# Transposing q and k of seven late units by the DMA instead of on TensorE

## The chip, the cores and the metric

One core of one Trainium2 chip. The metric is the device time of one execution in microseconds (us), lower is better. All times below are from runs of the fast state; where a kernel's time is given it is the median of its runs, and ratios to the kernel before come from runs of the same rounds on the same chip.

## The reference

Two blocks in series. A retention layer gives x, and a SiLU layer with two weight matrices takes it to the output. Everything is float32.

```
q, k, v: (batch 4, heads 8, seq 768, head_dim 64)
for t in range(S):
    state = gamma * state + outer(k[:, :, t], v[:, :, t])
    y[:, :, t] = scale * q[:, :, t] @ state
x = y as (3072 tokens, 512)
h = x @ w_in                 # (512, 2048)
out = (h * sigmoid(h)) @ w_out   # (2048, 512)
```

## The kernel before

The sequence is cut in 6 chunks of 128 tokens. A chunk of one batch is a *unit*: 24 units, numbered 0 to 23. For each unit a *visit* does the retention part in chunk form, with small matmuls that need q and k with head_dim on the partitions. So each visit begins by transposing q and k on TensorE, four 128x128 blocks each, and ScalarE copies them from PSUM:

```
def stage_t(n):                    # TensorE transposes k and q of unit n
    for name, to, bufs, src, tp in (("kt", kt, 2, kqv["k"][n], turn(...)),
                                    ("qt", qt, 3, kqv["q"].pop(n), banks("q", ...))):
        for a in range(HP):        # HP = 4 pairs of heads
            nc.tensor.transpose(tp[:, a, :], src[:, 2 * a : 2 * a + 2, :], ident)
        to[n] = one.tile([128, HP, C], FP32, ...)
        evac[:] = [nc.scalar.copy(out=to[n], in_=tp).ins]
```

Between the visits stand the *products*, h = x @ w_in for one chunk and one block of 128 columns of w_in: 96 in all, each 12 matmuls of 512 columns. ScalarE evacuates the first PSUM bank of a product (`ha`) into `hs`, VectorE subtracts the second (`hb`), ScalarE applies Silu, and SyncE sends `hs` to DRAM. There are three `hs` buffers:

```
hpool = pool("hpool", 3)
...
def product_in(c, f):
    ha, hb = turn(f"ha_{c}_{f}"), turn(f"hb_{c}_{f}")      # three banks in turn
    ... 12 matmuls ...
    hs = hpool.tile([128, NT], FP32, tag="hs", name=f"g_{c}_{f}")
    copied[:] = [nc.scalar.activation(out=hs, in_=ha, func=AF.Copy, scale=ONE_E).ins]
    ... what stands in behind_copy is placed here, on ScalarE's queue ...
    taken_out[:] = [nc.vector.tensor_tensor(out=hs, in0=hs, in1=hb, op=ALU.subtract).ins]
    ...
    nc.scalar.activation(out=hs, in_=hs, func=AF.Silu)
    pending.append((c, f, hs))

def put_g(keep):                    # the store of a product
    while len(pending) > keep:
        c, f, g = pending.pop(0)
        nc.sync.dma_start(out=g_dram[c, f], in_=g)

for n, (c, f) in enumerate(steps):
    product_in(c, f)
    if (c, f) in takes:
        take_w(...)                 # rounds a piece of w_out and stores it: load wf, store wod
    put_g(1)
    behind.get((c, f), lambda: None)()     # here the visits, one every four products later on
```

All loads and stores of this part are issued by SyncE, which takes them in one order. It is not always that of the text: a transfer that waits for nothing can stand far ahead of its place.

## Time and profile before

| | before |
|---|---|
| time, median of 4 runs | 634.22 us (632.36 to 634.83) |
| span of the profiled run | 633.9 us |
| TensorE busy, idle | 610.8, 23.1 us |
| DMA issues on SyncE, 209 to 321 us | 76, together 39.3 us of 112 (35%) |
| DMA packets of the run, those under 512 bytes | 123,215; 80,016 |

The lines behind these are in the prediction below.

### The profile page before, as it was taken

How to read it: one execution, taken by the hardware profiler on the slowest of the kernel's cores; microseconds unless marked ns; L12 is line 12 of the kernel's file. 1: busy time of each engine (PE TensorE's matmuls, PEld its weight loads, DVE VectorE, ACT ScalarE, POOL GpSimd, SP SyncE). 2: the span in 40 equal slices, each digit the busy share in tenths (PEclk: the TensorE clock that was granted, in tenths of full speed). 3: DMA queues.
4: the chain of work that ended last, by engine and by line, in shares of the span. 5: the costliest groups of instructions: out<-in, count | busy, mean ns of one | idle time of the engine just before them, and what ended most of it. 6: DMA issues, size and time to landing. Idle time of an engine off the chain costs nothing.

```text
span 633.9 us, 13555 instructions
## 1 busy us (share of the span) xinstructions
PE 610.8 (96%) x5440; PEld 506.1 (80%) x5440; DVE 420.9 (66%) x732; ACT 303.8 (48%) x583; POOL 7.1 (1%) x65
## 2 busy tenths in 40 slices
PE   5798999999999999999999999999999999999997
PEld 3686788887888888888888888888888888888785
DVE  2798897798968778687777675463645544554631
ACT  5568796676655546555467761221312221412311
POOL 3000000000000000000000000000000000000000
PEclk9989999999999999999999999999999999999999
DMA  9996886446667687775657644242433423342301
GB/s 197 213 203 174 214 228 228 166 149 200 201 196 205 177 239 224 210 218 189 231 188 216 207 139 132 100 159 73 157 109 98 170 75 124 133 131 90 112 0 67
DMA packets 123215, 103.65 MB, mean 164 GB/s; under 512 B 80016, under 2 KB 88464, under 8 KB 123152
## 3 DMA queue, kind: packets, MB, share of 16 engines
q1 hardware_dynamic: 120272, 97.54, 53.0%
q10 hardware_dynamic: 2880, 5.24, 2.2%
q8 instruction: 43, 0.70, 0.5%
q14 instruction: 20, 0.16, 0.1%
HBM read 66.06 MB, written 36.70 MB: 162 GB/s over the span
## 4 chain that ended last, share of the span: by engine, by line
PE 87%; DVE 4%; SPq 4%; DMA 2%; issue 1%; ACT 1%; DVEq 0%; ACTq 0%; POOLq 0%
PE ha L551 25%; PE o L696 20%; PE oa L696 14%; PE hb L551 13%; PE ob L696 7%; PE y L428 3%; SPq L145 3%; PE sc L395 1%; PE sc L385 1%; PE qp L369 1%; PE kp L369 1%; DMA gd<-g 1%; DMA kqv<-in_q_dram 1%; DMA wod<-cw 1%; SPq L167 0%
## 5 line engine op out<-in xcount | busy, mean ns | idle before, releaser
L551 PE MATMUL ha<-xt,wi 128*128 128x512 f32 x768 | 192.3, 392 | 0.4 <-ACT xt L475 0.4
L551 PEld LDWEIGHTS ha<-xt,wi 128*128 128x128 f32 x768 | 142.7, 188 | 31.0 <-ACT xt L475 0.5
L696 PE MATMUL o<-wo,gs 128*128 128x512 f32 x576 | 146.2, 389 | 0.0
L696 PEld LDWEIGHTS o<-wo,gs 128*128 128x128 f32 x576 | 108.1, 188 | 22.4
L608 DVE TENSOR_TENSOR gs<-gr,gs 128x512 fp32r<-128x512 f32 x96 | 62.1, 686 | 91.0 <-ACT gs L606 91.0
L696 PE MATMUL oa<-wo,gs 128*128 128x512 f32 x384 | 118.3, 389 | 0.0
L606 ACT ACTIVATE gs<-gr 128x512 fp32r<-128x512 f32 x96 | 53.4, 621 | 134.9 <-issue 132.5
L551 PE MATMUL hb<-xt,wi 128*128 128x512 f32 x384 | 103.2, 390 | 0.3 <-ACT g L555 0.2
L559 DVE TENSOR_TENSOR g<-g,hb 128x512 f32<-128x512 f32 x96 | 65.7, 684 | 42.0 <-ACT g L555 28.8
L551 PEld LDWEIGHTS hb<-xt,wi 128*128 128x128 f32 x384 | 71.7, 188 | 16.5 <-ACT g L555 1.0
L696 PEld LDWEIGHTS oa<-wo,gs 128*128 128x128 f32 x384 | 72.1, 188 | 14.9
L563 ACT ACTIVATE g<-g 128x512 f32<-128x512 f32 x96 | 60.6, 631 | 48.5 <-DVE g L559 48.2
L696 PE MATMUL ob<-wo,gs 128*128 128x512 f32 x192 | 75.3, 392 | 0.3 <-DVE o L705 0.3
L555 ACT ACTIVATE g<-ha 128x512 f32<-128x512 f32 x96 | 56.9, 593 | 32.5 <-PE ha L551 21.7
L609 DVE SCALAR_TENSOR_TENSOR gs<-gs 128x512 fp32r<-128x512 f32 x96 | 62.0, 684 | 0.0
L696 PEld LDWEIGHTS ob<-wo,gs 128*128 128x128 f32 x192 | 36.0, 188 | 9.3 <-DVE o L705 2.0
L193 ACT ACTIVATE ca<-wf 128x512 f32<-128x512 f32 x32 | 21.6, 676 | 9.5 <-DVE cs L200 4.6
L403 DVE TENSOR_TENSOR am<-sc,decay 128x512 f32<-128x512 f32 x24 | 16.5, 687 | 13.9 <-PE sc L395 13.7
L428 PE MATMUL y<-qt,mid 64*64 64x64 f32 x384 | 22.6, 231 | 1.9 <-issue 1.9
L200 DVE SCALAR_TENSOR_TENSOR cs<-ca,cs 128x512 uint32<-128x512 uint32 x32 | 22.1, 691 | 0.9
L204 DVE SCALAR_TENSOR_TENSOR cp<-wf,cp 128x512 f32<-128x512 uint32 x32 | 22.1, 689 | 0.6
L704 ACT ACTIVATE o<-o 128x512 f32<-128x512 f32 x10 | 6.0, 600 | 33.1 <-PE o L696 32.7
(80 smaller groups left out, 542.2 us busy)
## 6 DMA issues: line engine op xcount, KB each, us to landing
gd<-g SPq DMA_DIRECT2D x96, 256.0 KB, 3.1
gr<-gd SPq DMA_DIRECT2D x96, 256.0 KB, 2.8
wf<-in_moe_w_out_dram SPq DMA_DIRECT2D x16, 512.0 KB, 4.3
out_dram<-o ACTq DMA_DIRECT2D x20, 256.0 KB, 2.1
wf<-in_moe_w_in_dram SPq DMA_DIRECT2D x16, 256.0 KB, 3.6
wf<-in_moe_w_in_dram SPq DMA_DIRECT2D x32, 128.0 KB, 4.1
kf<-in_k_dram SPq DMA_DIRECT2D x16, 256.0 KB, 5.0
qf<-in_q_dram SPq DMA_DIRECT2D x16, 256.0 KB, 4.5
```

What stands on the lines that cost most here:

```text
L193: nc.scalar.activation(out=a.bitcast(FP32), in_=hi.bitcast(FP32), func=AF.Abs, scale=65536.0)
L200: nc.vector.scalar_tensor_tensor(out=s, in0=a, scalar=3, in1=s, op0=ALU.logical_shift_left, op1=ALU.bitwise_or)
L204: nc.vector.scalar_tensor_tensor(out=p.bitcast(FP32), in0=lo, scalar=2.0 ** -52, in1=p.bitcast(FP32), op0=ALU.mult, op1=ALU.mult)
L428: i = nc.tensor.matmul(yp[ts(e, D), o, a, :], lhsT=lhsT, rhs=rhs, start=(e, o) not in started, stop=True, skip_group_check=True).ins
L551: nc.tensor.matmul(hb if i == 2 else ha, lhsT=w_sb[f][:, i, ts(kk, 128)], rhs=xt[c][:, i, kk, :], start=kk == 0 and i != 1, stop=kk == KIN ...
L555: copied[:] = [nc.scalar.activation(out=hs, in_=ha, func=AF.Copy, scale=ONE_E).ins]
L559: taken_out[:] = [nc.vector.tensor_tensor(out=hs, in0=hs, in1=hb, op=ALU.subtract).ins]
L563: nc.scalar.activation(out=hs, in_=hs, func=AF.Silu)
L606: nc.scalar.activation(out=t[:, 0, :], in_=g, func=AF.Copy, scale=HALF)
L608: nc.vector.tensor_tensor(out=t[:, 1, :], in0=g, in1=high, op=ALU.subtract)
L609: nc.vector.scalar_tensor_tensor(out=t[:, 2, :], in0=t[:, 1, :].bitcast(FP32), scalar=-1.0 / EPS, in1=high, op0=ALU.mult, op1=ALU.add)
L696: nc.tensor.matmul(o, lhsT=g, rhs=wo[f][:, i, :], start=first_ and i != 1, stop=last and i != 0)
```

## The change

The intent is to take 56 transposes from the engine that bounds the kernel. For units 17 to 23, q and k go another way: gathered in DRAM (eight products ahead in the text; in the trace SyncE issues the gathers between 57.9 and 138.4 us), transposed by the DMA as 16-bit words two products ahead (a float32 has two of them, so each word plane ends in its own partitions), put in order by eight small SBUF-to-SBUF copies ("reorders"), and joined by a strided copy of 16-bit words on ScalarE, q's two products later and k's three. The load of q goes; k is still loaded as well, since other matmuls take it untransposed. Two tiles hold the transposed words (the tag `qf`), one for q and one for k.

```
+    def gather_t(n):
+        for name, src in (("q", q), ("k", k)):
+            t = dram.tile([128, H, D], FP32, ...)
+            nc.sync.dma_start(out=t, in_=src[b, :, ds(c * C, C)].rearrange("h t d -> t h d"))
+    def fetch_t(n):
+        for name in "qk":
+            t = ld.tile([128, H, C], U16, tag="qf", name=f"{name}w_{n}", bufs=2)
+            nc.sync.dma_start_transpose(
+                out=t, in_=rows.pop((name, n)).bitcast(U16).rearrange("t h w -> t (h w)"))
+    def order_t(n):
+        for name in "qk":
+            src = words.pop((name, n)).rearrange("p (a j) t -> p j a t", j=2)
+            t = ld.tile([128, 2, HP, C], U16, tag="kf", name=f"{name}p_{n}", bufs=3)
+            for w in range(2):
+                for j in range(2):
+                    nc.sync.dma_start(out=t[ts(j, D), w], in_=src[w::2, j])
+    def join_t(name, n):
+        nc.scalar.copy(out=to[n].bitcast(U16).rearrange("p a (t w) -> p w a t", w=2),
+                       in_=planes.pop((name, n)))
...
-        if first:
+        if first and m < FAR:                  # FAR = 17
             stage_t(m)
...
+        if n - 2 in far:                       # far: the products with the visits of 17 to 23
+            behind_copy.append(lambda m=far[n - 2]: join_t("q", m))
+        if n - 3 in far:
+            behind_copy.append(lambda m=far[n - 3]: join_t("k", m))
+            behind_next.append(lambda m=far[n - 3]: scale_k(m))
         product_in(c, f)
         ...
         put_g(1)
         behind.get((c, f), lambda: None)()
+        if n in far:
+            order_t(far[n])
+        if n + 2 in far:
+            fetch_t(far[n + 2])
+        if n + 8 in far:
+            gather_t(far[n + 8])
```

More of the change, by code (lines that the diff above doesn't have):

```diff
@@ L15 @@
 U32 = mybir.dt.uint32
+U16 = mybir.dt.uint16
 AF = mybir.ActivationFunctionType
@@ L129 @@
     EARLY = 2 * B
+    FAR = 4 * B + 1
     early = {}
@@ L360, in scale_q @@
         nc.vector.tensor_tensor(out=t, in0=t, in1=g, op=ALU.mult)
+    rows, words, planes = {}, {}, {}
+    def gather_t(n):
+        c, b = units[n]
+        for name, src in (("q", q), ("k", k)):
+            t = dram.tile([128, H, D], FP32, tag=f"{name}{n}", name=f"{name}d_{n}")
+            nc.sync.dma_start(out=t, in_=src[b, :, ds(c * C, C)].rearrange("h t d -> t h d"))
+            rows[name, n] = t
+    def fetch_t(n):
[3 more added lines that the diff above has]
+                out=t, in_=rows.pop((name, n)).bitcast(U16).rearrange("t h w -> t (h w)"))
+            words[name, n] = t
+    def order_t(n):
[5 more added lines that the diff above has]
+                    nc.sync.dma_start(out=t[ts(j, D), w], in_=src[w::2, j])
+            planes[name, n] = t
+    def join_t(name, n):
+        to, bufs = (qt, 3) if name == "q" else (kt, 2)
+        to[n] = one.tile([128, HP, C], FP32, tag=f"{name}t", name=f"{name}t_{n}", bufs=bufs)
+        nc.scalar.copy(out=to[n].bitcast(U16).rearrange("p a (t w) -> p w a t", w=2),
+                       in_=planes.pop((name, n)))
     def stage_t(n):
@@ L529, in visit @@
             first_chunk()
-        if first:
+        if first and m < FAR:
             scale_k(m)
@@ L535, in visit @@
         for name, n in (("k", m + 2), ("q", m + 2), ("v", m + 1)):
-            if n >= EARLY:
+            if n >= EARLY and (n < FAR or name == "v"):
                 load(name, n)
+        if m >= FAR:
+            load("k", m)
         if EARLY - 2 <= m < 3 * B + 2:
@@ L653 @@
     behind[1, NF - 1] = lambda: [late_x(3), visit(EARLY + 6)]
+    far = {steps.index(x): EARLY + 6 + i for i, x in enumerate(at)
+           if FAR <= EARLY + 6 + i < len(units)}
     for n, (c, f) in enumerate(steps):
+        if n - 2 in far:
[3 more added lines that the diff above has]
+            behind_next.append(lambda m=far[n - 3]: scale_k(m))
         product_in(c, f)
```

## The prediction

> **What bounds the kernel now.** I read the page's busy shares first, then a table of windows over the region that the change touches, then the chain of waits through one period, then the groups of the operations that go, and last the DMA and the waits. The page:
>
> ```profile
> PE 610.8 (96%) x5440; PEld 506.1 (80%) x5440; DVE 420.9 (66%) x732; ACT 303.8 (48%) x583; POOL 7.1 (1%) x65
> ...
> DMA  9996886446667687775657644242433423342301
> ```
>
> TensorE is busy 96% of the span; every other engine has room on average. An average hides stages, so the windows (us, then PE, PEld, DVE, ACT, POOL busy, clock, DMA share, GB/s):
>
> ```profile
> 0.00:30.00 30.00, 19.39 (x448) 15.68 (x448) 14.67 (x27) 17.01 (x44) 5.18 (x44) 0.94 1.05 203
> ...
> 209.00:223.00 14.00, 14.00 (x185) 11.86 (x184) 10.09 (x20) 6.94 (x12) 0.09 (x1) 1.00 0.62 190
> 223.00:237.00 14.00, 14.00 (x185) 11.82 (x184) 10.17 (x19) 7.06 (x12) 0.09 (x1) 1.00 0.84 241
> ...
> 251.00:265.00 14.00, 14.00 (x170) 11.82 (x168) 9.50 (x17) 8.15 (x16) 0.09 (x1) 1.00 0.80 233
> ...
> 365.00:400.00 35.00, 35.00 (x156) 29.00 (x155) 20.14 (x33) 13.09 (x24) 0.00 (x0) 1.00 0.39 121
> ```
>
> Units 14 to 23 are staged between about 179 and 291 us (the last transpose of k starts at 288.9). There PE never idles, DVE is at 70 to 85%, ACT at 50 to 60%. The DMA engines are the second resource: 62 to 84%, mean of the six 14-us windows from 209 to 293 0.72. One period of the chain of waits (start, length, what) reads:
>
> ```profile
> 257.90 1.81 PE ha L551 x8
> 259.71 0.91 PE hb L551 x4
> 260.62 0.44 PE kp L369 x4
> 261.06 0.44 PE qp L369 x4
> 261.50 0.63 PE y L428 x32
> ```
>
> Each product is 1.81 + 0.91 = 2.72 us of matmuls, back to back; every fourth is followed by a visit of 2.96 us (260.62 to 263.58), in which the eight transposes hold 0.44 + 0.44 = 0.88 us. All is on the chain, so whatever leaves PE here leaves the span, unless a new wait comes. The groups of what goes:
>
> ```profile
> L369 PE MATMUL kp<-ident,kf 128*128 128x128 f32 x64 | 9.7, 274 | 0.0
> L369 PE MATMUL qp<-ident,qf 128*128 128x128 f32 x64 | 9.6, 273 | 0.0
> L371 ACT COPY qt<-qp 128x512 f32<-128x512 f32 x24 | 14.0, 583 | 1.4 <-PE qp L369 1.4
> L371 ACT COPY kt<-kp 128x512 f32<-128x512 f32 x24 | 14.0, 582 | 6.8 <-PE kp L369 6.7
> ```
>
> A mean of 274 ns is a latency: four cost 0.44 us on the chain, 109 ns each, since they overlap. The 0.109, not the 0.274, is what can be won. Last, what is short of slack on the DMA side:
>
> ```profile
> ACT g L555 <- DMA gd<-g: 5.7, 4, 2.2
> ...
> gd<-g SPq DMA_DIRECT2D x96, 256.0 KB, 3.1
> ...
> qf<-in_q_dram SPq DMA_DIRECT2D x16, 256.0 KB, 4.5
> ```
>
> The first line says that ScalarE, evacuating a product, already waited four times (up to 2.2 us) for the store of an older product to free one of three buffers; PE did not notice, but the margin is small.
>
> **What the Trainium skill says.** (1) "DMA: Bandwidth & Descriptors", section "Latency and other measured facts", gives a DMA transpose 261 GB/s with a non-contiguous middle dimension and about 350 to 400 when contiguous. (2) "VectorE: DVE Perf Modes", section "The three transpose paths", gives 1309 ns for one 128x128 transpose of 2-byte elements by DMA. The kernel before has no DMA transpose, so no row supports either; they disagree for a large transfer (below). (3) The first page, section "Why small descriptors are slow (HBM only)", says that 256-byte descriptors lose time to HBM but not between SBUF and SBUF. The trace agrees on HBM: the loads of the first 30 us, 256 bytes a packet, ran 203 GB/s at a share of 1.05, so 193 GB/s at full share; the 2-KB traffic of 365 to 400 us ran 121 at 0.39, so 310. (4) "ScalarE: Activation LUTs", section "What ACT_TABLE_LOAD costs", gives an ACTIVATE with immediates 186 ns + 0.833 ns an element: 612 ns for 512 elements, and the trace's copies took 583.
>
> **The change part by part.** Seven units.
> - Removed on PE: 7 x 8 transposes at 109 ns, 7 x 0.88 = 6.1 us. All on the path. The k transposes also took a turn of the three product banks, so bank pressure falls a little; I count nothing for it. The 2.04 instead of 1.81 us of the first product after a visit stays: the small matmuls remain.
> - ScalarE: 14 copies of 0.58 us go, 14 copies of 1024 16-bit words come. Estimate from the ScalarE page: 186 + 0.833 x 1024 = 1.04 us each. Net 14 x 0.46 = +6.4 us over seven periods, 0.9 us on 13.1 with 50 to 60% busy: beside other work. A product's copy and Silu (0.59 + 0.63 us) with one join make 2.26 us, still under 2.72.
> - DMA work for each unit, in us of all 16 engines. Before: 0.72 x 14.0 = 10.1. Away: the q load, 0.262 MB at 193 GB/s, 1.36. New: two gathers DRAM to DRAM in 256-byte pieces, taken at the same rate, 2.7; two transposes, 0.524 MB at 261 GB/s, 2.0; eight reorderings of 64 KB within SBUF in 256-byte rows, 0.524 MB at 310 to 193 GB/s, 1.7 to 2.7. Net +5.0 to +6.0: 15.1 to 16.1 of work in a period that falls to 13.1 us. The gathers depend on nothing and may be issued long before their place: SyncE's order is not fixed as PE's is, and the late loads of y at 94 us stand some 20 products ahead of their place. In 110 to 165 us the DMA share is only about 0.5. Without the gathers the period asks 12.4 to 13.4 of 13.1: full, but hardly over.
> - SyncE for each period of four products: about 10 issues before (4 stores of products, 3 loads, 1.5 weight loads, 1.5 weight stores); 8 + 2 + 2 - 1 = 11 more. An issue took 0.32 to 0.38 us on an unloaded queue, and up to 2.7 us for a kf load when the queue was full. The eight reorderings are then a burst of 3 us or more in front of the next product's store.
> - Waits in order: transposes to reorderings two products (5.4 us), reorderings to q's join two products, to k's join three; a plain 256-KB load takes 4.5 to 5.0 us to land in this kernel. There is little to spare in the first two.
>
> Sum: -6.1 us if all transfers hide, 628.0 us. I charge an expected 3 us for periods in which ScalarE waits for a store or for the reordered words and PE idles: estimate 0.4 us a unit, from the store's margin of about 2 us against a burst of 3. 634.1 - 6.1 + 3.0 = 631.0 us.
>
> **The rivals.** (A) All hides: 628 us, 0.97% faster. For it: PE is the only bound there, the four waits for stores cost PE nothing, ScalarE has room. Against: DMA demand at or over 100% of the period. (B) A new wait takes the place of the gain: ScalarE is in order, so a join that waits for its words holds the next product's evacuation, and a store behind the reordering burst does the same. 0.5 to 1.5 us a unit gives 631 to 639. For it: the margin of 2 us and doubled issue count. (C) The DMA becomes the bound for seven periods: 15.1 to 16.1 against 13.1 would add 2 to 3 us a unit above the new pace, 642 to 649. For it: the sums above if gathers are not moved early, or if they are moved into the first 60 us, where the DMA share is about 1 and PE waits for loads. Against: weight staging for the output can slip. (D) The transpose runs at 1.3 us for each of its eight 128x128 blocks in series: 10.5 us for a transfer, 21 us a unit, over 14; that would block SyncE at the reorderings and cost 8 us a unit or more, beyond 680. Against: the bandwidth figure of the same skill, and sixteen engines share one transfer.
>
> **Range and chances.** More than 2% faster needs 12.7 us, twice all that is removed: 0.01. I give A 40%, B 35%, C 17%, D 8%. A and B and the mild half of C lie within 2% (up to 646.8): 0.80. Slower by over 2%: 0.19. The 8-in-10 range runs from just under the best case to the middle of C: 626.5 to 647.
>
> **What would show it.** Right: 56 fewer transposes of kp and qp; the visit on the chain 2.08 us instead of 2.96; PE idle nearly nil between 200 and 290 us; joins near 1.04 us; DMA share in that stretch 0.85 to 1.0. B would show as idle before the product's evacuation or the join, released by a DMA, with gaps in PE behind it. C would show DMA share about 1 for several periods with store landings of 6 us and more, or long stalls before 70 us. D would show a transpose's landing over 8 us and SyncE waiting for it. The prediction is wrong if the span is above 647, or if PE's idle time grows while every DMA lands as fast as before.

## More of the kernel before

The kernel's own weak spot can be seen in one group of its page, the second half of a product: it waited for ScalarE 0.2 us in the whole run.

```profile
L551 PE MATMUL hb<-xt,wi 128*128 128x512 f32 x384 | 103.2, 390 | 0.3 <-ACT g L555 0.2
```

## The result, and the profile after

652.50 us (652.15 to 653.04, 4 runs) against 634.22: slower. The ratio is 1.0294 (95% interval 1.0272 to 1.0317). Ratios are the mean time of one kernel's fast runs over that of the other's of the same rounds, so not quite the ratio of the medians. The result is correct. Times "above before" below are (ratio - 1) x 634 us, so here 18.6 us.

From the page after: TensorE's busy time, and the chain of work that ended last, by engine (87% of it was TensorE before, 2% DMA and 4% SyncE); then the group of the second half of a product.

```profile
PE 612.2 (94%) x5384; PEld 504.2 (77%) x5384; DVE 421.1 (65%) x732; ACT 313.0 (48%) x583; POOL 7.5 (1%) x65
...
PE 72%; DVE 8%; DMA 8%; SPq 6%; ACT 3%; issue 2%; ACTq 0%; DVEq 0%; POOL 0%; POOLq 0%
...
L592 PE MATMUL hb<-xt,wi 128*128 128x512 f32 x384 | 104.7, 395 | 13.7 <-ACT g L596 13.5
```

The 56 transposes are gone (5384 matmuls for 5440). But the group that waited 0.2 us now waits 13.5 us for L596, ScalarE's evacuation of the product before. TensorE idles 651.3 - 612.2 = 39.1 us instead of 23.1, so 16.0 us more. And its busy time went up by 1.4 where 6.1 us of work had left: 7.5 us is neither idle nor new work but slower matmuls. The windows of the kernel after show both (columns: length, busy of PE, PEld, DVE, ACT, POOL, granted clock, DMA share, GB/s):

```profile
195.00:209.00 14.00, 14.00 (x300) 11.80 (x299) 12.66 (x25) 7.78 (x16) 0.18 (x2) 1.00 0.81 162
209.00:223.00 14.00, 10.93 (x161) 8.97 (x160) 6.64 (x13) 7.27 (x11) 0.09 (x1) 0.89 0.88 230
...
265.00:279.00 14.00, 10.38 (x142) 8.45 (x141) 5.59 (x11) 6.61 (x9) 0.09 (x1) 0.88 0.95 236
279.00:293.00 14.00, 13.46 (x161) 10.55 (x159) 10.55 (x20) 8.14 (x12) 0.09 (x1) 1.00 0.89 231
293.00:307.00 14.00, 10.26 (x107) 8.03 (x110) 7.53 (x13) 6.77 (x10) 0.00 (x0) 0.82 0.95 209
```

In the windows where TensorE idles 3 us and more, the granted clock is 0.82 to 0.89; before it was 1.00 in each window from 195 to 335 us. Over the eight windows from 209 to 321 us the clock that was not granted adds up to 8.4 us of full speed, about the 7.5. So a gap here goes with slower work as well; that the gap is the reason for the lower clock is an inference, but run 14 below, whose gaps are nearly gone, has its clock back.

A second view gives the place. The 96 evacuations of the products follow one another in the same order in both kernels, so their starts can be subtracted. The kernel after is 1.4 us *ahead* of the kernel before up to product 45, 2.3 us ahead at product 47, behind by 1.5 at product 48 and by 17.0 at product 74, and stays there to the end. All that is lost, is lost between 209 and 321 us, where the seven units are staged. Moved by 1.4 + 17.0 = 18.4 us while the visits save 6.1, the stalls there cost 24.5 us.

What the product waited for, from the list of waits of the kernel after over its whole span (total us, times, longest):

```profile
ACT g L596 <- DMA gd<-g: 22.1, 14, 5.4
...
PE hb L592 <- ACT g L596: 13.5, 7, 3.7
...
ACT qt L398 <- DMA qp<-qw: 7.1, 4, 2.6
```

ScalarE waits for the store of an older product (`gd<-g`) to free a buffer, 22.1 us where it was 5.7, and now for the reordered words of q as well. The chain of waits through the first stall shows why the store is late (start, length, what):

```profile
210.39 0.39 SPq L173
...
211.31 0.63 SPq L391
...
211.98 0.65 SPq L391
...
212.67 0.64 SPq L391
...
213.35 0.66 SPq L391
...
214.12 3.44 DMA gd<-g
...
217.66 0.61 ACT g L596
```

The store was ready at 205.47 us, when its Silu ended, and was issued at 214.12: SyncE takes its DMAs in order and had other things to do first. The last of them are four reorders (L391), 0.63 to 0.66 us each, 2.7 us of the 8.65. Before them stood a transpose (1.26 us), a load of v (1.91, 1.6 of them a wait for TensorE) and the two transfers of w_out; and before these SyncE issued nothing until 206.89, because the transpose at its head had to wait until q's reorders of the unit before had landed. From SyncE's own list of waits, 197 to 215 us (total us, times, longest):

```profile
SPq L380 <- DMA qp<-qw: 3.2, 1, 3.2
```

Then the store took 3.44 us to land. Later periods are worse. This is SyncE's own timeline, where x4 is four issues:

```profile
237.90 5.80 SPq L391 DMA_DIRECT2D qp<-qw  x4
243.81 2.57 SPq L391 DMA_DIRECT2D kp<-kw  x4
246.49 1.32 SPq L610 DMA_DIRECT2D gd<-g  x2
...
248.98 1.56 SPq L380 DMA_TRANSPOSE qw<-qd  x1
250.64 3.42 SPq L380 DMA_TRANSPOSE kw<-kd  x1
```

Eight reorders hold SyncE 8.4 us and two transposes 5.0. The tile of q's words gives the durations of single issues (min, median, max in ns): a reorder takes 606 at least, a transpose of q 1265 at least, and both stretch:

```profile
L391 SPq DMA_DIRECT2D qp<-qw x28: 606/620/3746, 199.3 to 310.3; - x28
L380 SPq DMA_TRANSPOSE qw<-qd x7: 1265/1559/1939, 186.6 to 301.5; - x7
```

Summed from the trace, from 209 to 321 us SyncE issued 124 DMAs in 94.6 us, 84% of the time (before: 35%): 52 reorders 40.1 us, 11 transposes 21.3, 28 stores of products 15.3, the rest loads and w_out's two transfers. (About 4 us of these sums, in both kernels, are waits for an engine inside an issue.) The DMA engines' share rose there from 0.69 to 0.90, and the run's packets from 123,215 to 160,512, all of the increase under 512 bytes. So there are two suspects that go together: SyncE's queue, and the DMA engines behind it. The Trainium skill names both as ways to be DMA-bound ("Perfetto Trace Analysis", section "What 'DMA-bound' means": particular DMA engines, or the issuing engine's sequencer when its track is solid DMA slices). The trace fits either, which is what the experiments are for.

### The profile page after: what moved, and what is told of

Read it like the earlier page. It is cut to its first block, busy times and chain, and to the rows that moved or that the text cites. A ratio compares the mean times of both kernels' runs of the same rounds, so it can differ in the third digit from the quotient of the medians.

```text
span 651.3 us, 13527 instructions
## 1 busy us (share of the span) xinstructions
PE 612.2 (94%) x5384; PEld 504.2 (77%) x5384; DVE 421.1 (65%) x732; ACT 313.0 (48%) x583; POOL 7.5 (1%) x65
## 2 busy tenths in 40 slices
DMA packets 160512, 112.83 MB, mean 173 GB/s; under 512 B 117312, under 2 KB 125760, under 8 KB 160448
## 4 chain that ended last, share of the span: by engine, by line
PE 72%; DVE 8%; DMA 8%; SPq 6%; ACT 3%; issue 2%; ACTq 0%; DVEq 0%; POOL 0%; POOLq 0%
PE o L752 20%; PE ha L592 18%; PE oa L752 13%; PE hb L592 10%; PE ob L752 7%; DMA gd<-g 2%; PE y L467 2%; SPq L391 2%; SPq L149 2%; DMA yd<-ys 1%; SPq L380 1%; DMA wod<-cw 1%; DMA qp<-qw 1%; PE sc L424 1%; DMA wf<-in_moe_w_out_dram 1%
## 5 line engine op out<-in xcount | busy, mean ns | idle before, releaser
L592 PE MATMUL hb<-xt,wi 128*128 128x512 f32 x384 | 104.7, 395 | 13.7 <-ACT g L596 13.5
L596 ACT ACTIVATE g<-ha 128x512 f32<-128x512 f32 x96 | 56.7, 591 | 44.4 <-DMA gd<-g 22.1
L204 DVE SCALAR_TENSOR_TENSOR cs<-ca,cs 128x512 uint32<-128x512 uint32 x32 | 22.1, 690 | 0.8
```

The source lines that it names most:

```text
L204: nc.vector.scalar_tensor_tensor(out=s, in0=a, scalar=3, in1=s, op0=ALU.logical_shift_left, op1=ALU.bitwise_or)
L592: nc.tensor.matmul(hb if i == 2 else ha, lhsT=w_sb[f][:, i, ts(kk, 128)], rhs=xt[c][:, i, kk, :], start=kk == 0 and i != 1, stop=kk == KIN ...
```

## The experiments

Theory S: SyncE's time for issues is the cost; stores, weights and reorders wait for their turn. Theory D: the DMA engines' load is the cost; everything lands late, and SyncE's issues are only stretched by it. Theory G: the gathers in DRAM disturb the earlier part. The first rival within S was that only the *stores* suffer from standing behind the burst. The expectations count differently: theory 1 is S (in run 1 its narrow form, the stores), theory 2 is D, theory 3 is that the joins wait for their words, theory 4 that the transposes cost it, and theory 5 that each DMA has to wait for an older one whose completion semaphore it takes over.

| run | time | ratio to before, 95% | above before | correct |
|---|---|---|---|---|
| the change | 652.50 | 1.0294 (1.0272 to 1.0317) | 18.6 | yes |
| 1 stores from ScalarE | 653.14 | 1.0288 (1.0261 to 1.0315) | 18.3 | yes |
| 2 reorders of a quarter of the bytes | 643.79 | 1.0137 (1.0108 to 1.0166) | 8.7 | no |
| 3 plain copies for the transposes | 644.57 | 1.0145 (1.0113 to 1.0177) | 9.2 | no |
| 4 gathers alone | 635.67 | 1.0013 (0.9990 to 1.0035) | 0.8 | yes |
| 5 twice the reorders | 684.94 | 1.0774 (1.0736 to 1.0811) | 49.1 | yes |
| 6 reorders from GpSimd | 642.51 | 1.0112 (1.0081 to 1.0143) | 7.1 | yes |
| 7 reorders from ScalarE | 654.53 | 1.0299 (1.0257 to 1.0342) | 19.0 | yes |
| 8 q alone, k loaded early | 678.39 | 1.0686 (1.0639 to 1.0732) | 43.5 | yes |
| 9 runs 2 and 6 together | 639.75 | 1.0066 (1.0029 to 1.0103) | 4.2 | no |
| 10 q alone, k loaded later | 637.41 | 1.0019 (0.9977 to 1.0061) | 1.2 | yes |
| 11 run 10 with reorders from GpSimd | 637.01 | 1.0023 (0.9990 to 1.0055) | 1.5 | yes |
| 12 two small reorders per tensor | 640.63 | 1.0097 (1.0059 to 1.0134) | 6.1 | no |
| 13 run 10 with stores from ScalarE | 642.24 | 1.0097 (1.0058 to 1.0136) | 6.1 | yes |
| 14 runs 3 and 12 together | 634.17 | 0.9965 (0.9929 to 1.0001) | -2.2 | no |

Those marked "no" are wrong in their values: they keep the order of the work and take some of it away. Each diff is against the change; lines that only keep a run consistent (the size of the words' tile and a join that reads it broadcast in runs 2, 9, 12 and 14, a join that scales by 0.25 in runs 3 and 14, k's old way in runs 8, 10, 11 and 13) are left out.

**Run 4, the gathers alone** (the staging itself as before).

```
+    G0, FAR = FAR, len(units) + 9
-            if FAR <= EARLY + 6 + i < len(units)}
+            if G0 <= EARLY + 6 + i < len(units)}
...                              # and no fetch, order or join: "if n - 2 in far" -> "if 0", ...
```

> The kernel before with the seven pairs of DRAM-to-DRAM gathers added and nothing else (their result is not read). If the gathers hide in the slack from 57 to 140 us, as the trace of the changed kernel suggests, 632 to 637, the same as before. If they delay early loads, 637 to 645.

Measured 1.0013: 0.8 us above before, within the noise of 1.4. Theory G falls, as the product-by-product view said.

**Run 1, the stores of the products issued by ScalarE.**

```
-            nc.sync.dma_start(out=g_dram[c, f], in_=g)
+            nc.scalar.dma_start(out=g_dram[c, f], in_=g)
```

> The product stores are issued by ScalarE's queue instead of SyncE's; everything else is the changed kernel. Theory 1 (the stores stand behind the reorder and transpose issues in SyncE's in-order queue): stores go out right after Silu, ScalarE's waits for stores fall from 22 us to under 6, PE idle between 209 and 321 us mostly vanishes, span 628 to 637. Theory 2 (the 16 DMA engines are full, a store lands late whoever issues it): landings grow to 5 us and more, span 645 to 653. Theory 3 (joins wait for their words): span 643 to 650 with ScalarE's wait at the join unchanged at 7 to 10 us.

No gain at all. SyncE's share fell from 84 to 67%, and the waits for a product's store come to 2.5 us in the whole run. But the waits moved to the two transfers of w_out that still stand on SyncE, and to something that is named after k's words. From the list of waits, 195 to 330 us:

```profile
ACT ca L197 <- DMA wf<-in_moe_w_out_dram: 12.8, 3, 5.5
DVE cw L214 <- DMA wod<-cw: 11.7, 3, 5.1
...
ACT g L596 <- DMA kp<-kw: 10.4, 4, 4.6
```

In the kernel after the first two were 1.6 and 1.8 us in that stretch. The third line is not what its name says: a product's evacuation does not need k's words. The timeline of ScalarE shows what stood in front of it, the issue of a store that was ready when Silu ended:

```profile
240.30 0.63 ACT L604 ACTIVATE g<-g 128x512 f32<-128x512 f32 x1 [0.78 <-DVE g L600]
245.10 0.33 ACTq L610 DMA_DIRECT2D gd<-g  x1
245.53 0.60 ACT L596 ACTIVATE g<-ha 128x512 f32<-128x512 f32 x1 [4.59 <-DMA kp<-kw]
```

By the semaphores in the trace files, the DMAs of SyncE and ScalarE in this program complete on eight semaphores, taken in turn over both engines, and an issue waits until the older DMA on its semaphore has landed (theory 5). From 209 to 321 us that held up six stores on ScalarE for 11.0 us and nine issues on SyncE for 11.4 us; in the change it was one issue, 0.8 us. So run 1 brings in a wait of its own. It shows that moving the stores in this way gains nothing; it does not show whether the stores alone were the victims.

**Run 2, reorders with a quarter of the rows, eight issues as before; run 3, plain copies of 2-KB rows in place of the transposes.**

```
# run 2
-                    nc.sync.dma_start(out=t[ts(j, D), w], in_=src[w::2, j])
+                    nc.sync.dma_start(out=t[ts(j, D), w], in_=src[w::2, j, :1])
# run 3
-            nc.sync.dma_start_transpose(
-                out=t, in_=rows.pop((name, n)).bitcast(U16).rearrange("t h w -> t (h w)"))
+            nc.sync.dma_start(out=t, in_=rows.pop((name, n)).bitcast(U16))
```

> The same eight reorder DMAs for a unit, each moving a quarter of its rows (64 packets of 256 bytes instead of 256); the result is wrong on purpose. Theory 1 in its strict form (number of issues): issues stay eight, each about 0.35 us and more, span 640 to 652. Theory 2 (bytes and packets in the DMA engines): 1.5 thousand packets a unit fewer, span 630 to 638. If an issue's own length follows its descriptors, both share: issue 0.62 us falls to about 0.35 and the span lies at 634 to 642.

> The two transposes of a unit are plain copies of 2-KB rows, DRAM to SBUF, issued at the same places; the join scales by 0.25 so that the mixed words stay finite; the result is wrong on purpose. Theory 4 (the transposes cost it: 1.25 to 3.4 us of SyncE and 1024 packets each): span 630 to 638. Theory 1 with the reorders as the main part: half or less of the loss goes, 641 to 649.

Run 2 gave back (1.0294 - 1.0137) x 634 = 10.0 us, run 3 9.4 us: about half each of the 18.6, and neither theory alone. Run 2 separates bytes from issues less cleanly than meant. With a quarter of the packets the reorders' issues took 0.68 us in the mean (0.77 in the change), and the *transposes'* fell from 1.93 to 1.29: SyncE's issues from 209 to 321 us came to 84.7 us instead of 94.6, 9.9 us less, as much as the run gave back. So its gain need not be D's. Nor is it the load on the DMA engines that stretches an issue: the transposes' took 1.94 us in run 5 below at a DMA share of 0.69, and 1.28 to 1.40 in runs 1, 6 and 7 at 0.87 to 0.94. They were long in the two runs in which SyncE issues most densely (84 and 88% of the time; 38 to 67% in the other three). What stretches them is not shown.

**Run 5, the same bytes in sixteen reorders instead of eight.**

```
-                    nc.sync.dma_start(out=t[ts(j, D), w], in_=src[w::2, j])
+                    for a in range(0, HP, 2):
+                        nc.sync.dma_start(out=t[ts(j, D), w, a : a + 2],
+                                          in_=src[w::2, j, a : a + 2])
```

> Each of the eight reorder DMAs of a unit is split in two of half the rows: sixteen issues a unit, the same bytes and the same 256-byte packets; correct. Theory 1 (SyncE's issue time; an issue takes 0.6 us here) and theory 5 (eight completion semaphores in turn, so that each DMA waits for the eighth before it): about 4 to 5 us more SyncE time a unit, over a period that is already full, so 665 to 690. Theory 2 (the DMA engines' bytes and packets): nothing is added for them, 650 to 656.

30 us slower than the change, at no more bytes. This is theory S by itself: two windows of it show TensorE at 4.50 and 11.41 of 14 us while the DMA engines have *room*, 0.77 and 0.53 (0.74 to 1.04 in the change).

```profile
251.00:265.00 14.00, 4.50 (x76) 3.19 (x78) 3.76 (x8) 4.98 (x7) 0.00 (x0) 0.64 0.77 201
265.00:279.00 14.00, 11.41 (x116) 9.25 (x108) 8.91 (x16) 6.12 (x12) 0.09 (x1) 0.99 0.53 141
```

Theory 5, which expected the same time, falls by the trace: taking over a semaphore held SyncE up for 1.0 us in this stretch. A reorder of half the rows still took 0.593 us at least (0.606 with all, 0.465 with a quarter in run 2): the issue costs more by the piece than by the byte. 56 more of them at 0.6 us are 34 us of SyncE's time, near the 30 us lost, since SyncE had little left to give.

**Runs 6 and 7, the reorders issued by GpSimd or by ScalarE.**

```
-                    nc.sync.dma_start(out=t[ts(j, D), w], in_=src[w::2, j])
+                    nc.gpsimd.dma_start(out=t[ts(j, D), w], in_=src[w::2, j])      # run 6
+                    nc.scalar.dma_start(out=t[ts(j, D), w], in_=src[w::2, j])      # run 7
```

> The reorder DMAs are issued by GpSimd's queue; bytes unchanged; correct. SyncE loses 40 us of issues between 209 and 321. Theory 1: the stores and loads on SyncE go out in time, span 630 to 640. Theory 2: 646 to 653. A warning: GpSimd also sets the token that orders TensorE's products of the states, so if its queue is slow with these DMAs, TensorE waits there and the run tells little (655 and more, with waits for the token).

> The reorder DMAs are issued by ScalarE's queue, in its order; bytes unchanged; correct. Eight issues of about 0.6 us take 5 us of ScalarE a period of 13 us, on top of some 7.7. Theory 1: SyncE falls from 84% to about 50% of issue time; the loss moves to ScalarE, which now evacuates products late: 640 to 655. Theory 2: 650 to 660, with landings of stores as long as before.

GpSimd gave back 11.5 us: SyncE's share is 49%, and the stores are waited for 3.4 us instead of 18.8 from 195 to 330 us. ScalarE gave back nothing: SyncE's share falls to 38% there, but the reorders take 33.9 us of ScalarE's time between 209 and 321 us, and ScalarE is the engine that evacuates the products. As in run 1 the eight semaphores are shared as well, which held up ScalarE's issues for 13.2 us and SyncE's for 24.1; GpSimd's DMAs have semaphores of their own. In the 7.1 us left in run 6 three waits are seen. SyncE stands 23.1 us (195 to 321 us) before transposes, until reorders have landed and left the words' tiles. GpSimd now stands in line for the words' buffers, and the token that it passes to the small matmuls (a fence, one write per visit) waits behind; and at a DMA share of 0.85 to 1.09 (209 to 307 us) the weights land late. From the list of waits, 195 to 330 us:

```profile
ACT ca L197 <- DMA wf<-in_moe_w_out_dram: 8.6, 3, 3.5
...
DVE cw L214 <- DMA wod<-cw: 7.4, 3, 3.2
PE y L467 <- POOL token L339: 6.3, 9, 1.7
```

**Run 9, runs 2 and 6 together.**

```
-                    nc.sync.dma_start(out=t[ts(j, D), w], in_=src[w::2, j])
+                    nc.gpsimd.dma_start(out=t[ts(j, D), w], in_=src[w::2, j, :1])
```

> Both reliefs at once: the reorders go out from GpSimd and move a quarter of their rows; the result is wrong on purpose. Each alone gave back about half of the loss (643.8 and 642.5 against 652.5). If SyncE's issue time and the DMA engines' load are two causes that add up, the loss is gone but for the token waits of GpSimd (7 us seen): 630 to 637. If they are one cause seen twice (a queue that is long for either reason), nothing more is won: 640 to 644.

4.2 us above before, between the two expectations. Against run 6 a quarter of the reorders' bytes gains 2.9 us (1.0112 and 1.0066, and the intervals overlap); no other pair of runs comes as near to theory D by itself, so D's own part is small if it is there. ScalarE's wait for a product's store is gone (0.2 us), and TensorE's wait for GpSimd's token is 7.8 us in nine visits, 0.87 us each: as much as the eight transposes of a visit held. GpSimd is thus no free place for issues in this kernel.

**Run 12, two small reorders per tensor on SyncE, an eighth of the packets.**

```
-            for w in range(2):
-                for j in range(2):
-                    nc.sync.dma_start(out=t[ts(j, D), w], in_=src[w::2, j])
+            for j in range(2):
+                nc.sync.dma_start(out=t[ts(j, D), 0], in_=src[1::2, j, :1])
```

> All reorders stay on SyncE, but there are two for each of q and k instead of four, and each moves a quarter of its rows: four issues a unit and an eighth of the reorders' packets; the result is wrong on purpose. No GpSimd in it, so no token waits. If the reorders, by issue time on SyncE and load of the DMA engines together, are the whole cause: SyncE's share falls to about 0.6, TensorE idles under 5 us between 195 and 321, and the span is 629 to 634. If the two transposes of a unit (1.3 to 3.4 us of SyncE each and their own packets) are a third part of it: 635 to 640.

6.1 us above before, so 12.5 given back, and about half of the loss of 24.5 us is still there with nearly no reordering left. Its chain between 223 and 262 us shows the transfers that end the waits, each long in landing:

```profile
228.26 4.14 DMA gd<-g
...
235.28 7.18 DMA wf<-in_moe_w_out_dram
242.53 3.04 DMA gd<-g
249.91 5.88 DMA wod<-cw
```

What is left of the change beside the gathers are the transposes, the joins, and the wait of a transpose for the reorders before it, which now stops SyncE for 15.6 us between 195 and 321 us (4.6 in the change, none before).

**Run 14, runs 12 and 3 together: small reorders and no transposes.** Joins, gathers and order of issues stay.

```
-            nc.sync.dma_start_transpose(
-                out=t, in_=rows.pop((name, n)).bitcast(U16).rearrange("t h w -> t (h w)"))
+            nc.sync.dma_start(out=t, in_=rows.pop((name, n)).bitcast(U16))
-            for w in range(2):
-                for j in range(2):
-                    nc.sync.dma_start(out=t[ts(j, D), w], in_=src[w::2, j])
+            for j in range(2):
+                nc.sync.dma_start(out=t[ts(j, D), 0], in_=src[1::2, j, :1])
```

> The small reorders of run 12 and the plain fetch of run 3 together, wrong in its values on purpose: two small reorders per tensor, 14 fetches of 2-KB rows in place of the transposes; gathers, joins, loads and order of issues as in the change. Run 12 alone took 640.6, run 3 alone 644.6. If SyncE's time for the reorders and the transposes' own share are the whole of the loss, the saving on TensorE shows whole: 627 to 632 us, and SyncE's issues take under 55% of 209 to 321. If something that is still in it costs as well (the two small weights' loads behind a short queue, the lookahead of the stores, the 1.35-us joins), 634 to 639, and the waits that remain name it.

634.17 us, a ratio of 0.9965: 2.2 us under before by the ratio (its interval just holds 1), at the lower edge of what was expected for a third cause, and 20.9 us given back. Run 12 gave 12.5 and run 3 gave 9.4 alone, 21.9 together: the reorders and the transposes add up, and they are 21 of the 24.7 us (18.6 + 6.1) lost. SyncE's issues take 51%. The gaps are gone but for one window, and the clock is back at 1.00 with them:

```profile
251.00:265.00 14.00, 12.01 (x148) 9.47 (x147) 10.28 (x19) 9.31 (x16) 0.09 (x1) 0.88 0.73 230
265.00:279.00 14.00, 14.00 (x165) 11.55 (x164) 10.50 (x20) 8.19 (x14) 0.09 (x1) 1.00 0.78 222
```

The starts of the products, against the kernel before (us, minus is ahead), put the runs side by side:

| product | 45 | 47 | 48 | 56 | 62 | 74 | 95 |
|---|---|---|---|---|---|---|---|
| the change | -1.4 | -2.3 | 1.5 | 5.9 | 11.1 | 17.0 | 16.9 |
| run 12 | 1.1 | 0.2 | -0.1 | 4.2 | 6.5 | 5.5 | 4.7 |
| run 14 | -0.2 | -1.0 | -1.1 | -0.3 | 0.8 | -0.1 | -1.0 |

Run 14 still should have gone 6.1 us ahead between products 45 and 95 and went 0.8. Its waits in this stretch, for w_out's load (7.3 us), the stores (7.1) and w_out's rounded pieces (6.6), were 1.5, 3.5 and 0.9 in the kernel before. So some 4 to 5 us belong to neither the reorders' bulk nor the transposes. The 14 fetches, the 28 small reorders and the joins are what remains. SyncE's share of 51% hides a part of them: beside issuing, SyncE stands still before the fetches, with stores and w_out's transfers behind it, until the reorders of the unit before have left the words' tiles. From its list of waits, 195 to 321 us (the kernel before has none for a DMA there):

```profile
SPq L380 <- DMA qp<-qw: 8.2, 7, 2.1
SPq L380 <- DMA kp<-kw: 6.9, 2, 4.2
```

That makes this wait the likeliest holder of the rest, but no run takes it away (more tiles for the words would), and it stays open.

**Runs 8, 10, 11 and 13, q alone through the DMA, k still on TensorE.** They halve all that is added, for half of what is won (3.1 us). Run 8:

```
-        for name, src in (("q", q), ("k", k)):
+        for name, src in (("q", q),):
-        for name in "qk":            # in fetch_t and order_t
+        for name in "q":
-            if n >= EARLY and (n < FAR or name == "v"):
+            if n >= EARLY and (n < FAR or name != "q"):      # k is loaded two visits ahead
```

> Only q of units 17 to 23 takes the new way; k is loaded and transposed by TensorE as before: four reorders, one transpose, one gather a unit, and 28 transposes on TensorE go instead of 56 (7 x 0.44 = 3.1 us). If the loss sets in where the period is over-full (theories 1, 2 and 5 alike): SyncE and the DMA engines keep some slack, 631 to 636. If the loss is in proportion to the added work: half of 18 us, 641 to 645.

678.39 us, and the reason is an error of the experiment, not of the idea. The reordered words share the three buffers of k's loads, and with k loaded two visits ahead they had to wait until TensorE freed one, in the very visit that needed them:

```profile
PE sc L435 <- ACT qt L398: 33.8, 5, 7.4
```

Run 10 loads k one visit ahead instead; run 11 moves its reorders to GpSimd; run 13 moves its stores to ScalarE.

```
-        if m >= FAR:
-            load("k", m)
+        if m + 1 >= FAR:
+            load("k", m + 1)
```

> q alone, as in the run before of that name, with k loaded one visit ahead instead of two, so that three buffers of that tag are enough: in the run before, the reordered words had to wait for a buffer that TensorE freed only in the visit that needed them, and TensorE stood 7 us before the scores. If the loss sets in only where the period is over-full: 631 to 636. If it goes with the added work: 641 to 645.

> The same with its four reorders a unit issued by GpSimd. SyncE and DMA engines both have slack then; what remains is GpSimd's token, late by up to 2 us a unit. 631 to 637; below the kernel before only if the token waits stay under 3 us in all.

> A version that might beat the kernel before: q alone (mended), and the product stores issued by ScalarE, which leaves SyncE some 35 us of issues in 100 and lets the stores go out at once. 3.1 us less on TensorE, less what stays of late weights and of gathers in the first 100 us (2 to 3 us in the run of q alone). 632 to 637; not clear of the kernel before in either direction is the likeliest.

Runs 10 and 11 are level with before (1.0019 and 1.0023, both intervals hold 1). Between 209 and 321 us SyncE issues for 51% of the time in run 10 and for 33% in run 11, and in both the 3.1 us won are gone, so what is left is not issue time alone. Run 13 is slower than run 10 by 4.8 us: 31 stores took 10.2 us of ScalarE's time between 209 and 321 us. That this costs more than it frees on SyncE is a possible reason, but no run tests it by itself, and by the starts of the products 4.5 of the 8.1 us that run 13's profiled run loses are lost before product 45. No correct version that ran beats the kernel before. A fourth `hs` buffer, which would let a store be late, was tried in a build and did not fit into SBUF (a later pool needs 8 KB a partition and 6.5 are left), so it was not run.

## Why the prediction was wrong

By its own steps:

- **Removed on PE, 6.1 us.** Right. 56 matmuls fewer; at the first visit without transposes, between products 45 and 46, the kernel after gained 0.87 us against the 0.88 predicted.
- **ScalarE, +6.4 us beside other work.** Mis-sized, with no consequence that shows. A join took 1.35 us against the estimate of 1.04, so 14 x 0.31 = 4.3 us more; ScalarE is busy 6.6 to 8.2 us of 14 in these windows. Its order does matter: q's joins wait 9.4 us for words (7.1 for q's own, 2.3 for k's), and a product's evacuation stands behind each.
- **DMA work, a share of 0.85 to 1.0.** Right: 0.90. The gathers were issued early, as assumed, and cost nothing (run 4). One reading was mixed: the 193 GB/s taken for 256-byte packets holds 1,024 packets of 1 KB as well, and by the packets' own times the 19,451 of 256 bytes ran at 184. That changes the sum by under 0.2 us a unit.
- **SyncE, 11 more issues in a period, at 0.32 to 0.38 us: a burst of "3 us or more".** The count was right and the duration wrong, and this is where the prediction failed first. A reorder takes 0.59 us at least and 0.77 in the mean, a transpose 1.23 at least and 1.93 in the mean, so in place of 10 x 0.35 = 3.5 us the ten take 8 x 0.77 + 2 x 1.93 = 10.0 us. The row taken for it was that of plain 256-KB stores on an unloaded queue; the transposes had no row before. SyncE went from 35 to 84% busy, an account that the prediction never drew up: it counted issues, and did not hold their sum against the period.
- **Waits in order.** The prediction held each transfer against the one that needs its data. It left out the wait the other way: a transpose waits, at the head of SyncE's queue, until the reorders before it have left the tile that it writes. In the change this stops SyncE for 4.6 us from 195 to 321 us, 3.2 of them in front of the first late store; in runs 6, 12 and 14, where SyncE has fewer or shorter issues, for 15.1 to 23.1.
- **The stalls, "an expected 3 us", 0.4 us a unit.** This is the term of the sum that failed. It measured 24.5 us, 3.5 us a unit. The mechanism named beside it, a store behind the burst of reorders and ScalarE in order behind the store, is on the chain, so rival B had the right cause with the wrong size, "0.5 to 1.5 us a unit". But the burst of 3 us is only a part of what a store stands behind: for the first late store it was 2.7 us of 8.65. Run 5 shows the term growing with the number of issues at constant bytes, run 2 shows it falling by 10.0 us with the bytes and with SyncE's issue time, run 14 shows that reorders and transposes hold most of it, and runs 6 and 9 show that taking them off SyncE's queue leaves other waits.
- **The gaps' price.** Not in the prediction. Of the 23.5 us that the profiled runs show, 16.0 are idle and 7.5 are slower work, in and after the gaps, where the granted clock was lower (8.4 us of clock not granted).
- **Rivals C and D.** C came nearest in time (642 to 649 against 652.5), for the wrong reason: run 5 loses most at a DMA share of 0.53 to 0.79, which a bound of the DMA engines can't do. D did not occur: a transpose landed in 5.3 us (q) and 5.6 us (k) in the median, not in 10.5.

So the range (626.5 to 647.0) missed by 5.5 us, since its upper end followed from C's DMA sums and not from the queue in front of them.

## What to carry to other kernels

Before moving work to the DMA, add up the *issues*: for each period, number times duration of one issue of that very kind, on the engine that issues them, and compare the sum with the period, as for any other engine. Add what the queue stands still for as well, above all tiles that an earlier transfer must leave first: SyncE issued for 51% of the time in run 14, and stores and loads were still late. What is saved on the bounding engine must be larger than the margin with which its buffers come free, or a small saving buys a large stall, and slower work after it. When a late store is the wait, look first for what stands in front of it, and before moving it to another queue, check what the new queue shares with the old one: in run 1 it was the completion semaphores.

## What the Trainium skill lacked or had wrong

- "DMA: Bandwidth & Descriptors", section "Issuing engines are not separate DMA queues", says that the sequencer's time to initiate a DMA is usually small relative to the DMA. Not here: 124 issues took SyncE 94.6 of 112 us, and moving the reorders to GpSimd alone gave back 11.5 us (run 6). Beside cycle counts for "previous generations" in a table on trn3, the page gives no duration of an issue by kind. Measured here: 0.32 us for a plain 256-KB store at best, 0.59 to 0.61 for a 64-KB SBUF-to-SBUF reorder, 1.23 for a transpose, and up to 3.7 on a loaded queue.
- "Perfetto Trace Analysis", section "What 'DMA-bound' means", recommends large descriptors where the issuing sequencer is the bound. Here the number of DMAs mattered at constant packet size and bytes: halving each reorder and doubling their number cost 30 us (run 5), a reorder's issue being 0.593 us at least with half the rows and 0.606 with all.
- "DMA: Bandwidth & Descriptors", section "Latency and other measured facts", gives a transpose 261 GB/s, which is 1.0 us for 256 KB as an estimate. No run shows that rate by itself; in the change a transpose landed in 5.3 to 5.6 us in the median, much like a plain load of the same stretch (5.1 to 5.5 us), and in 3.2 to 3.4 us where SyncE was less dense (runs 10 to 12). The 1309 ns per 128x128 block of "VectorE: DVE Perf Modes", section "The three transpose paths", does not add up over the eight blocks of such a transfer (10.5 us).
- "ScalarE: Activation LUTs", section "What ACT_TABLE_LOAD costs", gives an ACTIVATE 186 ns + 0.833 ns an element. For a copy of 1024 16-bit words written with a stride of two words that is 1.04 us; it took 1.35 us.
